# Another order for one hand-written schedule: linear-attention block and ReLU MLP, 542 operations

## The chip, the core and the metric

The kernel runs on one core of a Trainium2 chip. The metric is the device time of one execution in microseconds (us). Engines named below: PE (TensorE matmuls; PEld its weight loads), DVE (VectorE), ACT (ScalarE), POOL (GpSimd) and SP (SyncE, here the one that issues every DMA). Each engine works through its own instructions in the order in which the program emits them; semaphores hold an instruction until what it reads is there and what it overwrites is free.

## The reference

Both stages work on the same x (2048 tokens, 512 features); B_x is not used.

```python
def _A_ref(x, wqkv, wo):                       # 32 heads of 16
    qkv = (x @ wqkv).reshape(B, S, 3, H, Dh).transpose(2, 0, 3, 1, 4)
    q, k, v = qkv[0], qkv[1], qkv[2]
    phi = lambda t: jnp.where(t > 0, t + 1, jnp.exp(t)) + 1e-6
    pq, pk = phi(q), phi(k)
    kv = jnp.einsum("bhsd,bhse->bhde", pk, v)
    z = jnp.einsum("bhsd->bhd", pk)
    num = jnp.einsum("bhqd,bhde->bhqe", pq, kv)
    den = jnp.einsum("bhqd,bhd->bhq", pq, z)[..., None] + 1e-6
    return (num / den).transpose(0, 2, 1, 3).reshape(B, S, D) @ wo

def _B_ref(x, w1, w2):                         # 512 -> 1792 -> 512
    return jnp.maximum(x @ w1, 0) @ w2

h = x + _A_ref(_layernorm(x), wqkv, wo)
h2 = h + _B_ref(_layernorm(h), w1, w2)
```

## The kernel before

The 2048 rows are 16 tiles t of 128, four tiles to a chunk c of 512 columns. The program is a set of small operations (`op_...`) and one string, `ORDER`, with 542 words; a word names an operation and its numbers, and the loop at the end emits them one after another:

```python
for word in ORDER.split():
    name, *idx = word.split(".")
    ops[name](*map(int, idx))
```

So the order of the words is the order on every engine's queue, and nothing else sets it. The last number of a PE word is its PSUM bank of eight.

What the words do, by stage:

- Loads, on SP: `lx.t.n` loads n tiles of x; `lk`, `lq`, `lv`, `lo`, `l1`, `l2` load rows of wk, wq, wv, wo, w1 and w2 (L200 to L211).
- `warm.n.b`: n products of zeros on PE (L215).
- First layernorm: `S.t` and `A.t` on DVE (statistics, L218, L219), `R.t.n` on ACT (1/sqrt as exp of a logarithm, two instructions, L224, L225), `N.t` on DVE (normalise, L243).
- Transposing normalised rows into `lnT`: tiles 0 to 3 with `T.t.b` on PE (L262) and `E.t` on ACT (L272); tiles 4 to 15 with `X.t`, a transposing DMA issued on SP (L283).
- Keys: `K.t.b` on PE (four matmuls, L291), then `F` (exp) and `U` (relu) on ACT (L309, L312) and `M`, `D` on DVE (min, add; L316, L319) make phi(k), one or two tiles at once. `G.t` (four matmuls into banks 4 to 7, L343) sums phi(k)^T ln(x) over all tiles; `za` and `zf` on DVE and `z` on PE sum phi(k).
- Queries: `Q.c.j.b` on PE (four matmuls, L299), `qF`, `qU`, `qM`, `qD` as for the keys.
- `gD` (DVE, L379) or `gA` (ACT, L376) copies G's banks out; `kv`, `kx`, `m` make one 512 by 512 matrix of kv and wo, copied out by `mA` (ACT) or `mD` (DVE).
- Denominators: `dn.c.b` on PE (16 small matmuls, L440), `dnl`, `dnx` on ACT (logarithm and exp, L446, L453), `dt.t`, a transposing DMA on SP (L460), into `rd`, and `dm` on DVE (L464), which multiplies phi(q) by it, two of four feature blocks at once.
- `h.t.b` on PE (four matmuls, L474), `hD.t` on DVE (adds x, L480); second layernorm with `s`, `a`, `n` on DVE (L220, L221, L250) and `r` on ACT; `x.t`, a transposing DMA on SP (L284).
- MLP: `p.c.f.b` on PE (four matmuls, L490), copied out with relu, two f at once, by `pA` (ACT, L496) or `pD` (DVE, L501); `f.t.b.f0.n` on PE (n matmuls of the sum over 14, L510); `fo.t` on DVE (scale and add, L518); `fd.t` on SP (store, L525). The activations lie in `acts[c % 2]`.

For one chunk the path is thus: four `dt` (after `dn`, `dnl`, `dnx`), two `dm`, four `h`, `hD`, `s`, `a`, `n`, four `x`, then `p`.

Of the kernel before, what the change touches and what calls it, by code (L numbers as in the profile page):

```python
# [15 lines left out]


ORDER = """
const lx.0.1 S.0 lx.2.1 S.2 lx.1.1 A.2 A.0 table warm.9.7 R.2.1 S.1 lx.3.1 N.2 A.1 R.0.1 R.1.1 N.0 lx.4.2
warm.1.7 T.2.0 S.3 E.2 N.1 T.0.1 A.3 lk.0.2 lk.2.2 S.4 S.5 A.4 lx.6.2 A.5 T.1.5 E.0 R.3.1 E.1 R.4.2 lx.8.4 N.3  # L20
K.0.3 S.6 N.4 F.0.1 U.0.1 K.1.0 lx.12.4 M.0.1 S.7 N.5 F.1.1 X.4 A.6 D.0.1 M.1.1 A.7 T.3.5 E.3 K.2.3 S.9 U.1.1
F.2.1 R.6.2 K.3.2 G.0 D.1.1 U.3.1 N.7 X.5 S.8 X.7 N.6 A.8 M.2.1 A.9 U.2.1 R.8.2 F.3.1 S.10 D.2.1 G.1 N.8 K.4.0
masks S.11 N.9 A.10 A.11 M.3.1 K.5.1 G.2 X.6 U.4.2 R.10.2 X.8 K.7.3 F.4.2 K.6.2 S.13 D.3.1 X.9 G.3 N.11 S.12
M.4.2 A.12 A.13 N.10 K.8.0 K.9.1 D.4.2 X.11 R.12.2 G.4 F.6.2 N.12 N.13 S.14 U.6.2 S.15 za.2 A.14 A.15 M.6.2
G.5 K.11.3 X.10 U.8.2 F.8.2 K.10.2 R.14.2 X.13 X.12 M.8.2 D.6.2 lq.0.2 lq.2.2 N.14 K.13.1 D.8.2 za.4 K.12.0
U.10.2 F.10.2 M.10.2 N.15 D.10.2 za.6 G.6 U.12.2 F.12.2 X.14 G.7 G.8 Q.0.1.1 Q.0.0.0 X.15 M.12.2 za.8 D.12.2
K.14.2 K.15.3 qU.0.0.2 qF.0.0.2 za.10 G.9 za.12 Q.0.2.0 Q.0.3.1 F.14.2 l1.2.2 M.14.2 U.14.2 zf.12 qF.0.2.2
D.14.2 G.10 G.11 z.0.2.14 z.2.2.14 z.1.2.14 qM.0.2.2 qM.0.0.2 z.3.2.14 qU.0.2.2 qD.0.2.2 lv.2.2 l2.7.7 lv.0.2
zc G.12 qD.0.0.2 G.13 zh dn.0.0 G.14 G.15 dnl.0 dnx.0.2.2 gD.0.2 Q.1.0.2 Q.1.1.3 dnx.0.0.2 gA.2.2 kv.0.4
Q.1.2.0 kv.3.4 Q.1.3.1 kv.2.4 qF.1.0.2 qU.1.0.2 qM.1.0.2 lo.2.2 lo.0.2 kv.1.4 kx Q.2.1.3 qF.1.2.2 dt.2 dt.3  # L30
dt.0 dt.1 qU.1.2.2 m.0.4 m.1.5 m.3.7 m.2.6 Q.2.0.2 qM.1.2.2 mA.0.2 qD.1.0.2 qD.1.2.2 dn.1.5 mA.2.2 dnl.1
dnx.1.2.2 dm.0.0.2 dm.0.2.2 h.3.4 h.2.0 hD.3 s.3 l1.0.2 dnx.1.0.2 hD.2 dt.6 a.3 Q.2.3.1 h.0.5 s.2 dt.4 hD.0
qU.2.0.2 qF.2.0.2 Q.2.2.0 qM.2.0.2 h.1.2 dt.5 dt.7 s.0 n.3 a.2 hD.1 a.0 s.1 n.0 Q.3.1.3 a.1 n.2 qF.2.2.2
qU.2.2.2 qM.2.2.2 dm.1.0.2 Q.3.0.2 dm.1.2.2 n.1 Q.3.3.1 Q.3.2.0 x.3 qF.3.0.2 qU.3.0.2 h.7.4 h.6.5 x.0 x.2
qU.3.2.2 qD.2.2.2 x.1 qD.2.0.2 dn.2.3 dnl.2 qF.3.2.2 h.5.6 h.4.7 hD.7 qM.3.0.2 hD.6 hD.5 s.7 p.0.0.2 p.0.1.3
hD.4 qM.3.2.2 s.6 dnx.2.2.2 dnx.2.0.2 pD.0.0.2 qD.3.2.2 s.4 dt.10 p.0.3.1 p.0.2.0 p.0.4.2 p.0.5.3 pA.0.2.2
pA.0.4.2 qD.3.0.2 dt.8 dt.11 dt.9 dn.3.6 p.0.6.0 p.0.7.1 p.0.13.3 dnl.3 s.5 a.4 p.0.12.2 pA.0.6.2 dnx.3.0.2
pA.0.12.2 r.0.4 dnx.3.2.2 l2.0.7 a.5 n.5 a.7 dm.2.0.2 a.6 n.6 dm.2.2.2 n.7 x.7 h.11.4 h.9.6 h.8.1 h.10.5 hD.11
n.4 hD.9 hD.8 hD.10 x.4 dt.13 dt.12 x.6 x.5 dt.14 dt.15 p.0.10.0 f.2.6.0.7 p.0.11.1 pA.0.10.2 p.0.8.2 p.0.9.3
f.3.7.0.7 pD.0.8.2 s.8 dm.3.0.2 dm.3.2.2 f.2.6.7.7 p.1.0.0 p.1.1.1 f.3.7.7.7 h.12.3 pD.1.0.2 h.14.4 p.1.2.2  # L40
p.1.12.0 hD.12 s.12 fo.3 fo.2 s.10 a.12 s.9 hD.14 s.11 a.9 n.9 h.13.7 f.1.5.0.7 p.1.13.1 h.15.3 a.10 hD.13 a.8
n.10 pD.1.12.2 n.8 hD.15 s.15 p.1.10.6 p.1.11.7 f.0.4.0.7 p.1.3.3 p.1.8.0 f.0.4.7.7 a.15 p.1.9.1 fd.2
f.1.5.7.7 pD.1.2.2 s.13 n.15 pA.1.8.2 fo.1 a.11 n.12 n.11 pD.1.10.2 x.8 x.9 x.10 x.11 p.1.4.0 p.1.5.1 p.1.6.2
r.4.4 p.1.7.3 pA.1.4.2 pA.1.6.2 f.5.5.0.7 p.2.3.3 p.2.8.0 p.2.9.1 f.7.7.0.7 p.2.2.2 pD.2.8.2 fo.0 p.2.1.1
p.2.0.0 f.6.6.0.7 s.14 a.13 n.13 pD.2.2.2 pD.2.0.2 a.14 p.2.7.3 f.4.4.0.7 p.2.12.0 p.2.6.2 f.7.7.7.7 p.2.13.1
n.14 f.5.5.7.7 pD.2.6.2 pA.2.12.2 p.2.5.1 p.2.4.0 x.13 fd.0 fd.3 x.15 fd.1 pA.2.4.2 x.14 x.12 f.4.4.7.7
p.3.0.0 p.3.2.2 p.3.1.1 f.6.6.7.7 p.3.3.3 pA.3.2.2 pD.3.0.2 fo.7 fo.5 fo.6 fo.4 p.3.9.1 f.11.7.0.7 p.2.11.3
fd.4 p.3.8.0 p.2.10.2 f.9.5.0.7 pD.2.10.2 pD.3.8.2 p.3.6.2 p.3.7.3 f.9.5.7.7 f.10.6.0.7 pA.3.6.2 p.3.10.2
p.3.11.3 f.8.4.0.7 fd.6 fd.5 fd.7 p.3.4.0 f.10.6.7.7 p.3.5.1 f.11.7.7.7 f.8.4.7.7 pA.3.4.2 r.12.4 r.8.4
pD.3.10.2 fo.9 fo.10 fo.8 fo.11 p.3.12.0 p.3.13.1 pD.3.12.2 fd.9 fd.8 fd.10 fd.11 f.14.6.0.7 f.13.5.0.7  # L50
f.12.4.0.7 f.14.6.7.7 f.13.5.7.7 f.12.4.7.7 fo.13 fo.14 fo.12 fd.12 fd.14 f.15.7.0.14.0.2 fo.15.0.2
f.15.4.0.14.2.1 f.15.5.0.14.3.1 fo.15.2.1 fo.15.3.1 fd.13 fd.15.0.2 fd.15.2.1 fd.15.3.1
"""


# [505 lines left out]
```

## Time and profile before

| what | us |
|---|---|
| median of 3 runs (lowest, highest) | 171.69 (171.44, 172.59) |
| the profiled execution | 171.47 |
| its span, first to last instruction | 169.8 |
| DVE / ACT busy | 103.3 / 64.9 |
| DMA packets of the program, share of 16 engines | 35.8% |

The page shows each engine's busy time, then the span in 40 slices (a digit is the busy tenths of a slice). These rows of it tell of DMA: the busy share of the 16 DMA engines by slice, and the queues. `q1` carries all that SP issues; `q8` and `q14` carry the fetches of the engines' own instructions, in packets of 16 KB and 8 KB. They run on the same 16 DMA engines.

```profile
DMA  5874466891556434564400131004500210003004
q1 hardware_dynamic: 32224, 15.74, 35.8%
q8 instruction: 6, 0.10, 0.2%
q14 instruction: 4, 0.03, 0.1%
```

By the packet records the six 16 KB packets start at 21.97, 44.68, 63.33, 88.23, 115.85 and 142.85 us and take 0.88 to 1.68 us each on one DMA engine; the 8 KB packets start at 16.62, 43.08, 77.35 and 86.58 and take 0.31 to 0.49.

The timeline of SP with all its transposing DMAs: a line has start, length of the merged stretch, line, kind, tensors and count.

```profile
10.27 14.38 SPq L283 DMA_TRANSPOSE lnT<-h_nat  x10
25.90 3.19 SPq L283 DMA_TRANSPOSE lnT<-h_nat  x2
41.40 6.19 SPq L460 DMA_TRANSPOSE rd<-wk_sb  x4
50.71 5.12 SPq L460 DMA_TRANSPOSE rd<-wk_sb  x4
55.92 5.15 SPq L284 DMA_TRANSPOSE lnT<-hn  x4
```

SP is held about 1.2 us by one transposing DMA, and the median from issue to landing is 2.5 us.

### The profile page before, as it was taken

The page shows a single profiled execution, that of the slowest core. Times are in us where ns is not written, and L with a number is a line of the kernel's source. Part 1 is how long each engine was busy: PE and PEld are TensorE (multiplying, and loading weights), DVE is VectorE, ACT ScalarE, POOL GpSimd, SP SyncE. Part 2 cuts the span into 40 slices and gives each one's busy share as a digit, 9 for nine tenths or more (in the row PEclk, how much of TensorE's full clock was granted, in tenths as well). Part 3 has the DMA queues.
Part 4 walks back from the last instruction along what each step waited for, and adds up shares of the span by engine and source line. Part 5 has one row for each costly group of instructions (what it writes and reads, how often), then busy time and mean ns, then how long its engine had stood idle before and what let it go on. Part 6 is the DMA issues. An engine that isn't in the chain of part 4 may idle for free.

```text
span 169.8 us, 2263 instructions
## 1 busy us (share of the span) xinstructions
PE 162.2 (96%) x843; PEld 75.4 (44%) x858; DVE 103.3 (61%) x206; ACT 64.9 (38%) x97; POOL 4.7 (3%) x21
## 2 busy tenths in 40 slices
PE   7799899999989999999999999999999999999993
...
DVE  3989999995269999770499845093203550227052
...
DMA  5874466891556434564400131004500210003004
GB/s 144 251 253 95 94 95 184 262 359 60 99 174 165 93 66 85 152 173 86 92 6 31 31 62 29 2 0 107 113 0 0 70 54 4 0 0 124 0 4 120
DMA packets 32234, 15.87 MB, mean 93 GB/s; under 512 B 24800, under 2 KB 31200, under 8 KB 32224
## 3 DMA queue, kind: packets, MB, share of 16 engines
q1 hardware_dynamic: 32224, 15.74, 35.8%
q8 instruction: 6, 0.10, 0.2%
q14 instruction: 4, 0.03, 0.1%
HBM read 7.86 MB, written 2.10 MB: 59 GB/s over the span
## 4 chain that ended last, share of the span: by engine, by line
PE 80%; DMA 6%; DVE 6%; SPq 2%; issue 2%; ACT 1%; DVEq 0%
PE bk L510 29%; PE bk L490 28%; PE bk L474 7%; PE bk L343 7%; PE bk L291 5%; PE bk L299 5%; DMA x_nat<-in_A_x_dram 3%; DMA lnT<-h_nat 2%; DVE h_nat L480 2%; DMA rd<-wk_sb 1%; SPq L201 1%; DVE st L220 1%; DVE h_nat L243 1%; PE bk L440 1%; ACT eb L309 1%
## 5 line engine op out<-in xcount | busy, mean ns | idle before, releaser
L510 PE MATMUL bk<-w_sb,at 128*128 128x512 bf16 (+2 forms) x249 | 51.9, 355 | 0.2
L490 PE MATMUL bk<-lnT,w_sb 128*128 128x512 bf16 x219 | 51.8, 379 | 0.2
L496 ACT ACTIVATE at<-bk 128x1024 bf16<-128x1024 f32 x13 | 13.3, 1024 | 70.6 <-PE bk L490 48.7
L501 DVE TENSOR_SCALAR at<-bk 128x1024 bf16<-128x1024 f32 x15 | 18.2, 1220 | 32.5 <-PE bk L490 32.3
L510 PEld LDWEIGHTS <-at 128*128 128x128 bf16 x252 | 23.6, 98 | 25.4 <-ACT at L496 0.3
L490 PEld LDWEIGHTS <-w_sb 128*128 128x128 bf16 x224 | 21.8, 98 | 26.1 <-issue 0.2
L518 DVE SCALAR_TENSOR_TENSOR gT<-bk,rstd,h_nat 128x512 bf16<-128x512 f32 (+2 forms) x18 | 11.7, 685 | 16.0 <-PE bk L510 10.5
L312 ACT ACTIVATE rb<-bk 128x1024 bf16<-128x1024 f32 (+1 forms) x18 | 16.4, 927 | 3.7 <-PE bk L299 2.4
L309 ACT ACTIVATE eb<-bk 128x1024 bf16<-128x1024 f32 (+1 forms) x18 | 16.6, 927 | 3.0 <-PE bk L299 2.8
L291 PE MATMUL bk<-wk_sb,lnT 128*128 128x512 bf16 x63 | 15.6, 379 | 1.3 <-DMA wk_sb<-in_A_wqkv_dram 0.6
L474 PE MATMUL bk<-m_sb,pqs 128*128 128x512 bf16 x61 | 15.0, 379 | 0.9 <-DVE pqs L464 0.8
L299 PE MATMUL bk<-lnT,wq_sb 128*128 128x512 bf16 x64 | 15.6, 379 | 0.2 <-DVE h_nat L480 0.2
L343 PE MATMUL bk<-at,h_nat 128*128 128x512 bf16 x54 | 13.3, 379 | 0.1
L480 DVE TENSOR_TENSOR h_nat<-bk,x_nat 128x512 bf16<-128x512 f32 x16 | 10.9, 681 | 2.0 <-PE bk L474 1.9
L218 DVE BATCH_NORM_STATS2 st<-x_nat 128x6 f32<-128x512 bf16 x16 | 10.6, 674 | 2.4 <-DMA x_nat<-in_A_x_dram 2.4
L220 DVE BATCH_NORM_STATS2 st<-h_nat 128x6 f32<-128x512 bf16 x16 | 11.0, 686 | 0.1
L291 PEld LDWEIGHTS <-lnT 128*128 128x128 bf16 x64 | 5.8, 98 | 9.5 <-DMA lnT<-h_nat 1.8
L474 PEld LDWEIGHTS <-pqs 128*128 128x128 bf16 x64 | 6.0, 98 | 8.0 <-DVE pqs L464 1.5
L299 PEld LDWEIGHTS <-wq_sb 128*128 128x128 bf16 x64 | 6.1, 98 | 7.2 <-issue 0.4
L343 PEld LDWEIGHTS <-h_nat 128*128 128x128 bf16 x64 | 6.1, 98 | 7.1
L316 DVE TENSOR_SCALAR eb<-eb 128x1024 bf16<-128x1024 bf16 (+1 forms) x18 | 6.8, 384 | 2.5 <-ACT eb L309 2.5
L453 ACT ACTIVATE wk_sb<-ld 128x1024 bf16<-128x1024 f32 x8 | 8.1, 1049 | 0.1
...
## 6 DMA issues: line engine op xcount, KB each, us to landing
...
```

Source lines behind the costliest of these rows:

```text
L220: op_s = lambda t: nc.vector.bn_stats(out=st2[:, t, :], in_=h_nat[:, t, :])
L291: nc.tensor.matmul(bk[:, b, :], lhsT=lnT[c][:, kd, j * P : (j + 1) * P], rhs=wk_sb[:, kd, :], start=(kd == 0), stop=(kd == KD - 1),)
L299: nc.tensor.matmul(bk[:, b, :], lhsT=wq_sb[:, kd, j * P : (j + 1) * P], rhs=lnT[c][:, kd, :], start=(kd == 0), stop=(kd == KD - 1),)
L309: nc.scalar.activation(out=buf(eb, kind, i, n), in_=bank(at_bank[kind, i], n), func=ACT.Exp)
L312: nc.scalar.activation(out=buf(rb, kind, i, n), in_=bank(at_bank[kind, i], n), func=ACT.Relu)
L343: nc.tensor.matmul(bk[:, KD + kd, :], lhsT=ln_nat[:, t, kd * P : (kd + 1) * P], rhs=pk(t)[:, 0, :], start=(t == 0), stop=(t == NT - 1),)
L474: nc.tensor.matmul(bk[:, b, :], lhsT=pqs[:, (c * KD + jb) % NQ, j * P : (j + 1) * P], rhs=m_sb[:, jb, :], start=(jb == 0), stop=(jb == KD ...
L480: nc.vector.tensor_tensor(out=h_nat[:, t : t + n, :], in0=bank(at_bank["h", t], n), in1=x_nat[:, t : t + n, :], op=ALU.add,)
L490: nc.tensor.matmul(bk[:, b, cols], lhsT=w1_sb[:, kd, f * P : (f + 1) * P], rhs=lnT[c][:, kd, cols], start=(kd == 0), stop=(kd == KD - 1),)
L496: nc.scalar.activation(out=acts[c % 2][:, f : f + n, :], in_=bank(at_bank["p", c, f], n), func=ACT.Relu)
L501: nc.vector.tensor_scalar(out=acts[c % 2][:, f : f + n, :], in0=bank(at_bank["p", c, f], n), scalar1=0.0, scalar2=None, op0=ALU.max,)
L510: nc.tensor.matmul(bk[:, b, 0 : w * P], lhsT=acts[c % 2][:, f, j * P : (j + 1) * P], rhs=w2_sb[:, f, k * P : (k + w) * P], start=(f == 0), ...
```

## The change

Only the string `ORDER` changes. Both versions have 542 words and the same work. Some copies change engine: `gA.2.2` (ACT) becomes `gD.2.2` (DVE), `mA.2.2` becomes `mD.2.2`, and of the 28 relu copies of the MLP ten go from `pD` to `pA` and four from `pA` to `pD`. Some `T`, `K` and `h` products use other PSUM banks. All else is where the words stand. The whole diff, its unchanged lines left out:

```diff
-const lx.0.1 S.0 lx.2.1 S.2 lx.1.1 A.2 A.0 table warm.9.7 R.2.1 S.1 lx.3.1 N.2 A.1 R.0.1 R.1.1 N.0 lx.4.2
-warm.1.7 T.2.0 S.3 E.2 N.1 T.0.1 A.3 lk.0.2 lk.2.2 S.4 S.5 A.4 lx.6.2 A.5 T.1.5 E.0 R.3.1 E.1 R.4.2 lx.8.4 N.3
-K.0.3 S.6 N.4 F.0.1 U.0.1 K.1.0 lx.12.4 M.0.1 S.7 N.5 F.1.1 X.4 A.6 D.0.1 M.1.1 A.7 T.3.5 E.3 K.2.3 S.9 U.1.1
-F.2.1 R.6.2 K.3.2 G.0 D.1.1 U.3.1 N.7 X.5 S.8 X.7 N.6 A.8 M.2.1 A.9 U.2.1 R.8.2 F.3.1 S.10 D.2.1 G.1 N.8 K.4.0
-masks S.11 N.9 A.10 A.11 M.3.1 K.5.1 G.2 X.6 U.4.2 R.10.2 X.8 K.7.3 F.4.2 K.6.2 S.13 D.3.1 X.9 G.3 N.11 S.12
-M.4.2 A.12 A.13 N.10 K.8.0 K.9.1 D.4.2 X.11 R.12.2 G.4 F.6.2 N.12 N.13 S.14 U.6.2 S.15 za.2 A.14 A.15 M.6.2
-G.5 K.11.3 X.10 U.8.2 F.8.2 K.10.2 R.14.2 X.13 X.12 M.8.2 D.6.2 lq.0.2 lq.2.2 N.14 K.13.1 D.8.2 za.4 K.12.0
-U.10.2 F.10.2 M.10.2 N.15 D.10.2 za.6 G.6 U.12.2 F.12.2 X.14 G.7 G.8 Q.0.1.1 Q.0.0.0 X.15 M.12.2 za.8 D.12.2
-K.14.2 K.15.3 qU.0.0.2 qF.0.0.2 za.10 G.9 za.12 Q.0.2.0 Q.0.3.1 F.14.2 l1.2.2 M.14.2 U.14.2 zf.12 qF.0.2.2
-D.14.2 G.10 G.11 z.0.2.14 z.2.2.14 z.1.2.14 qM.0.2.2 qM.0.0.2 z.3.2.14 qU.0.2.2 qD.0.2.2 lv.2.2 l2.7.7 lv.0.2
-zc G.12 qD.0.0.2 G.13 zh dn.0.0 G.14 G.15 dnl.0 dnx.0.2.2 gD.0.2 Q.1.0.2 Q.1.1.3 dnx.0.0.2 gA.2.2 kv.0.4
-Q.1.2.0 kv.3.4 Q.1.3.1 kv.2.4 qF.1.0.2 qU.1.0.2 qM.1.0.2 lo.2.2 lo.0.2 kv.1.4 kx Q.2.1.3 qF.1.2.2 dt.2 dt.3
-dt.0 dt.1 qU.1.2.2 m.0.4 m.1.5 m.3.7 m.2.6 Q.2.0.2 qM.1.2.2 mA.0.2 qD.1.0.2 qD.1.2.2 dn.1.5 mA.2.2 dnl.1
-dnx.1.2.2 dm.0.0.2 dm.0.2.2 h.3.4 h.2.0 hD.3 s.3 l1.0.2 dnx.1.0.2 hD.2 dt.6 a.3 Q.2.3.1 h.0.5 s.2 dt.4 hD.0
-qU.2.0.2 qF.2.0.2 Q.2.2.0 qM.2.0.2 h.1.2 dt.5 dt.7 s.0 n.3 a.2 hD.1 a.0 s.1 n.0 Q.3.1.3 a.1 n.2 qF.2.2.2
-qU.2.2.2 qM.2.2.2 dm.1.0.2 Q.3.0.2 dm.1.2.2 n.1 Q.3.3.1 Q.3.2.0 x.3 qF.3.0.2 qU.3.0.2 h.7.4 h.6.5 x.0 x.2
-qU.3.2.2 qD.2.2.2 x.1 qD.2.0.2 dn.2.3 dnl.2 qF.3.2.2 h.5.6 h.4.7 hD.7 qM.3.0.2 hD.6 hD.5 s.7 p.0.0.2 p.0.1.3
-hD.4 qM.3.2.2 s.6 dnx.2.2.2 dnx.2.0.2 pD.0.0.2 qD.3.2.2 s.4 dt.10 p.0.3.1 p.0.2.0 p.0.4.2 p.0.5.3 pA.0.2.2
-pA.0.4.2 qD.3.0.2 dt.8 dt.11 dt.9 dn.3.6 p.0.6.0 p.0.7.1 p.0.13.3 dnl.3 s.5 a.4 p.0.12.2 pA.0.6.2 dnx.3.0.2
-pA.0.12.2 r.0.4 dnx.3.2.2 l2.0.7 a.5 n.5 a.7 dm.2.0.2 a.6 n.6 dm.2.2.2 n.7 x.7 h.11.4 h.9.6 h.8.1 h.10.5 hD.11
-n.4 hD.9 hD.8 hD.10 x.4 dt.13 dt.12 x.6 x.5 dt.14 dt.15 p.0.10.0 f.2.6.0.7 p.0.11.1 pA.0.10.2 p.0.8.2 p.0.9.3
-f.3.7.0.7 pD.0.8.2 s.8 dm.3.0.2 dm.3.2.2 f.2.6.7.7 p.1.0.0 p.1.1.1 f.3.7.7.7 h.12.3 pD.1.0.2 h.14.4 p.1.2.2
-p.1.12.0 hD.12 s.12 fo.3 fo.2 s.10 a.12 s.9 hD.14 s.11 a.9 n.9 h.13.7 f.1.5.0.7 p.1.13.1 h.15.3 a.10 hD.13 a.8
-n.10 pD.1.12.2 n.8 hD.15 s.15 p.1.10.6 p.1.11.7 f.0.4.0.7 p.1.3.3 p.1.8.0 f.0.4.7.7 a.15 p.1.9.1 fd.2
-f.1.5.7.7 pD.1.2.2 s.13 n.15 pA.1.8.2 fo.1 a.11 n.12 n.11 pD.1.10.2 x.8 x.9 x.10 x.11 p.1.4.0 p.1.5.1 p.1.6.2
-r.4.4 p.1.7.3 pA.1.4.2 pA.1.6.2 f.5.5.0.7 p.2.3.3 p.2.8.0 p.2.9.1 f.7.7.0.7 p.2.2.2 pD.2.8.2 fo.0 p.2.1.1
-p.2.0.0 f.6.6.0.7 s.14 a.13 n.13 pD.2.2.2 pD.2.0.2 a.14 p.2.7.3 f.4.4.0.7 p.2.12.0 p.2.6.2 f.7.7.7.7 p.2.13.1
-n.14 f.5.5.7.7 pD.2.6.2 pA.2.12.2 p.2.5.1 p.2.4.0 x.13 fd.0 fd.3 x.15 fd.1 pA.2.4.2 x.14 x.12 f.4.4.7.7
-p.3.0.0 p.3.2.2 p.3.1.1 f.6.6.7.7 p.3.3.3 pA.3.2.2 pD.3.0.2 fo.7 fo.5 fo.6 fo.4 p.3.9.1 f.11.7.0.7 p.2.11.3
-fd.4 p.3.8.0 p.2.10.2 f.9.5.0.7 pD.2.10.2 pD.3.8.2 p.3.6.2 p.3.7.3 f.9.5.7.7 f.10.6.0.7 pA.3.6.2 p.3.10.2
-p.3.11.3 f.8.4.0.7 fd.6 fd.5 fd.7 p.3.4.0 f.10.6.7.7 p.3.5.1 f.11.7.7.7 f.8.4.7.7 pA.3.4.2 r.12.4 r.8.4
-pD.3.10.2 fo.9 fo.10 fo.8 fo.11 p.3.12.0 p.3.13.1 pD.3.12.2 fd.9 fd.8 fd.10 fd.11 f.14.6.0.7 f.13.5.0.7
-f.12.4.0.7 f.14.6.7.7 f.13.5.7.7 f.12.4.7.7 fo.13 fo.14 fo.12 fd.12 fd.14 f.15.7.0.14.0.2 fo.15.0.2
-f.15.4.0.14.2.1 f.15.5.0.14.3.1 fo.15.2.1 fo.15.3.1 fd.13 fd.15.0.2 fd.15.2.1 fd.15.3.1
+const lx.2.1 S.2 lx.0.1 lx.1.1 S.0 S.1 A.0 A.1 A.2 lx.4.2 table lx.3.1 R.0.1 S.3 N.0 R.2.1 R.1.1 A.3 R.3.1
+warm.9.7 N.1 N.2 warm.1.7 N.3 T.0.6 S.5 lk.0.2 lk.2.2 S.4 T.1.3 T.2.4 E.0 T.3.1 K.0.7 A.5 lx.6.2 A.4 E.1 E.2
+E.3 R.4.2 F.0.1 S.7 S.6 K.1.4 F.1.1 K.3.2 N.4 K.2.1 N.5 A.7 M.1.1 M.0.1 A.6 U.0.1 U.1.1 R.6.2 D.0.1 F.2.1
+D.1.1 N.7 N.6 lx.8.4 lx.12.4 U.2.1 F.3.1 S.8 S.9 X.4 X.5 M.3.1 A.8 M.2.1 A.9 X.6 G.0 G.1 K.4.0 U.3.1 D.3.1
+D.2.1 X.7 R.8.2 K.5.1 G.2 N.9 X.9 G.3 K.6.2 U.4.2 F.4.2 K.7.3 N.8 S.10 S.12 S.13 A.12 M.4.2 A.13 R.12.2 K.9.1
+F.6.2 X.8 U.6.2 S.14 S.11 N.12 D.4.2 A.11 A.10 M.6.2 N.13 X.12 X.13 K.8.0 R.10.2 F.8.2 D.6.2 G.4 N.10 A.14
+S.15 N.11 X.10 X.11 A.15 za.2 M.8.2 U.8.2 lq.0.2 lq.2.2 G.5 za.4 D.8.2 masks G.6 G.7 K.12.0 K.13.1 R.14.2 N.15
+X.15 za.6 N.14 za.8 U.12.2 F.12.2 K.10.2 K.11.3 G.8 F.10.2 U.10.2 M.12.2 M.10.2 D.10.2 G.9 X.14 Q.0.1.1
+Q.0.0.0 D.12.2 za.10 qF.0.0.2 qU.0.0.2 K.14.2 K.15.3 G.10 Q.0.2.0 za.12 zf.12 U.14.2 F.14.2 M.14.2 Q.0.3.1
+G.11 G.12 qF.0.2.2 D.14.2 qU.0.2.2 z.0.2.14 z.1.2.14 z.2.2.14 z.3.2.14 qM.0.0.2 qM.0.2.2 qD.0.2.2 G.13 zc
+qD.0.0.2 lo.2.2 lv.0.2 l2.0.7 lv.2.2 l1.0.2 lo.0.2 zh G.14 dn.0.0 G.15 dnl.0 gD.0.2 gD.2.2 dnx.0.2.2 Q.1.1.3
+Q.1.0.2 dnx.0.0.2 Q.1.2.0 qF.1.0.2 kv.1.4 dt.3 qU.1.0.2 Q.1.3.1 qM.1.0.2 qF.1.2.2 kv.2.4 kv.0.4 kv.3.4 Q.2.1.3
+qD.1.0.2 kx m.0.4 m.1.5 m.3.7 m.2.6 dt.1 dt.2 dt.0 qU.1.2.2 qM.1.2.2 Q.2.0.2 qD.1.2.2 mD.2.2 dm.0.0.2 mA.0.2
+dn.1.5 Q.2.3.1 dm.0.2.2 h.3.7 hD.3 dnl.1 h.0.6 s.3 dnx.1.2.2 l1.2.2 h.2.5 Q.2.2.0 hD.0 h.1.6 dt.7 dnx.1.0.2
+qU.2.0.2 qF.2.0.2 Q.3.0.2 Q.3.1.3 hD.2 qF.2.2.2 qU.2.2.2 a.3 s.0 s.2 n.3 a.0 a.2 hD.1 n.0 n.2 dt.5 dt.6 dt.4
+s.1 dm.1.0.2 x.3 dm.1.2.2 x.2 x.0 qM.2.0.2 a.1 Q.3.2.0 Q.3.3.1 n.1 qF.3.0.2 qU.3.2.2 qF.3.2.2 qU.3.0.2
+qM.2.2.2 qD.2.0.2 qD.2.2.2 h.7.7 h.5.4 h.6.6 h.4.5 dn.2.3 dnl.2 x.1 p.0.0.2 hD.7 hD.5 qM.3.2.2 hD.6 s.7 hD.4
+p.0.1.3 dnx.2.2.2 dnx.2.0.2 p.0.2.0 p.0.3.1 pA.0.0.2 qM.3.0.2 a.7 qD.3.2.2 pA.0.2.2 p.0.5.3 p.0.4.2 pA.0.4.2
+r.0.4 s.4 qD.3.0.2 n.7 l2.7.7 dt.11 s.6 dt.10 dt.8 dt.9 dn.3.6 p.0.7.1 p.0.6.0 pA.0.6.2 dnl.3 a.6 s.5 dm.2.0.2
+a.4 p.0.12.2 p.0.13.3 a.5 n.5 dm.2.2.2 pA.0.12.2 p.0.10.0 f.2.6.0.7 p.0.11.1 dnx.3.2.2 n.4 pD.0.10.2 n.6
+dnx.3.0.2 r.4.4 x.5 dt.14 x.7 dt.13 dt.12 dt.15 x.4 x.6 p.0.9.3 p.0.8.2 h.11.7 pA.0.8.2 h.9.4 h.10.2 f.1.5.0.7
+f.1.5.7.7 f.2.6.7.7 h.8.3 p.1.1.1 p.1.0.0 dm.3.0.2 hD.11 hD.9 hD.10 fo.2 dm.3.2.2 s.9 s.10 fo.1 hD.8 pA.1.0.2
+p.1.2.2 h.13.7 h.15.4 hD.13 h.14.5 p.1.13.1 p.1.12.0 pD.1.12.2 p.1.3.3 f.3.7.0.7 s.13 pD.1.2.2 h.12.0 s.11
+hD.15 hD.14 a.10 a.11 hD.12 s.8 n.11 a.8 a.9 f.3.7.7.7 f.0.4.0.7 p.1.9.1 p.1.8.0 p.1.6.2 p.1.10.6 p.1.7.3
+pA.1.8.2 fd.2 fd.1 r.8.4 s.15 n.8 s.12 a.13 a.12 n.10 n.13 fo.3 s.14 n.9 pD.1.6.2 a.14 p.1.5.1 p.1.4.0
+p.1.11.7 f.0.4.7.7 x.8 pA.1.4.2 x.10 x.9 x.11 fd.3 n.14 pD.1.10.2 fo.0 f.7.7.0.7 p.2.2.2 p.2.8.0 p.2.3.3
+f.4.4.0.7 p.2.9.1 pA.2.8.2 pD.2.2.2 f.5.5.0.7 p.2.1.1 p.2.7.3 f.7.7.7.7 f.4.4.7.7 f.6.6.0.7 p.2.0.0 p.2.6.2
+pA.2.0.2 f.6.6.7.7 p.2.4.0 a.15 fo.7 n.12 pD.2.6.2 p.2.5.1 p.2.11.3 r.12.4 pA.2.4.2 fo.6 fd.0 f.11.7.0.7
+p.2.10.2 p.2.13.1 p.2.12.0 pA.2.12.2 fo.4 n.15 fd.7 x.14 x.15 fd.4 x.13 x.12 f.5.5.7.7 f.8.4.0.7 p.3.9.1
+p.3.8.0 fo.5 pA.2.10.2 pA.3.8.2 fd.5 fd.6 p.3.2.2 f.10.6.0.7 p.3.4.0 f.9.5.0.7 p.3.3.3 p.3.5.1 f.10.6.7.7
+pA.3.4.2 p.3.1.1 pD.3.2.2 p.3.6.2 f.11.7.7.7 p.3.0.0 p.3.7.3 f.9.5.7.7 pD.3.6.2 pA.3.0.2 p.3.10.2 f.8.4.7.7
+p.3.11.3 p.3.13.1 fo.10 fo.11 fo.9 f.13.5.0.7 f.14.6.0.7 p.3.12.0 pA.3.12.2 pA.3.10.2 fo.8 f.12.4.0.7
+f.13.5.7.7 f.14.6.7.7 fd.8 fd.11 fd.10 fd.9 f.12.4.7.7 fo.13 fo.12 fo.14 f.15.7.0.14.0.2 f.15.5.0.14.3.1
+fo.15.0.2 fd.13 fd.12 fd.14 fd.15.0.2 fo.15.3.1 f.15.4.0.14.2.1 fo.15.2.1 fd.15.3.1 fd.15.2.1
```

## The prediction

> **What bounds the kernel now.** First the page: the busy time and the slices.
>
> ```profile
> PE 162.2 (96%) x843; PEld 75.4 (44%) x858; DVE 103.3 (61%) x206; ACT 64.9 (38%) x97; POOL 4.7 (3%) x21
> PE   7799899999989999999999999999999999999993
> DVE  3989999995269999770499845093203550227052
> ```
>
> PE is the bound, and from slice 15 (4.24 us each) it is full. All that an order can win lies before that, so I read next PE's timeline from 5 to 57 us, the lines with idle time in front of them:
>
> ```profile
> 6.98 0.40 PE L262 MATMUL bk<-ident,h_nat 128*128 128x128 bf16 x4 [0.52 <-DVE h_nat L243]
> ...
> 8.54 1.46 PE L291 MATMUL bk<-wk_sb,lnT 128*128 128x512 bf16 x6 [0.63 <-DMA wk_sb<-in_A_wqkv_dram]
> ...
> 18.03 1.04 PE L291 MATMUL bk<-wk_sb,lnT 128*128 128x512 bf16 x4 [0.52 <-DMA lnT<-h_nat]
> ...
> 49.84 1.84 PE L474 MATMUL bk<-m_sb,pqs 128*128 128x512 bf16 x7 [0.81 <-DVE pqs L464]
> ...
> 56.16 1.02 PE L299 MATMUL bk<-lnT,wq_sb 128*128 128x512 bf16 x4 [0.16 <-DVE h_nat L480]
> ```
>
> The brackets count from the modelled end of the last matmul. By start-to-start times (a 512-column matmul follows the last after 0.216 us, so K, Q, G, h or p, four each, cost 0.864) the waits are 0.68 (T.1), 0.79 (K.0 for its weights), 0.37 (K.2, K.3), 0.68 (K.6), 0.17 (K.12), 1.11 (h.3), 0.32 (Q.3.0): 4.1 us between T.2 at 5.68 and p.0.0 at 62.62. After p.0.0 there is none (steps of twice 0.216 every 50 matmuls are missing records). Of these, 1.96 hang on a transposing DMA (K.6, K.12, h.3).
>
> Third, the chain of waits from 43 to 50 us, and the DMA answers for one microsecond and one transpose there:
>
> ```profile
> 45.33 0.94 SPq L460
> 46.28 0.04 issue
> 46.32 2.47 DMA rd<-wk_sb
> 48.79 0.03 DVEq L464
> 48.82 0.05 issue
> 48.87 0.70 DVE pqs L464
> 49.57 0.27 issue
> 49.84 0.38 PE bk L474
> ```
>
> ```profile
> q8 instruction: 1, 0.02, 7.3%
> ```
>
> ```profile
> rd<-wk_sb SPq DMA_TRANSPOSE x1, 4.3
> ```
>
> The second fence is the microsecond from 44.5: one 16 KB instruction packet, 7.3% of 16 engines' 1.0 us, so 1.17 us on one of them. The third is dt.3, issued at 42.63: 4.3 us to landing where the median is 2.5. dt.0 behind it (43.99) holds SP 2.28 us instead of 1.2, so dt.1 goes out 1.05 late, lands at 48.79, and PE idles. The same at 21.97 (X.10 4.1 us, X.13 2.08 on SP) and, smaller, at 16.62 with an 8 KB packet (X.6 3.39). A 16 KB packet costs a train of transposes about 1.0 us, an 8 KB one about 0.9 to one landing. The 16 KB packets follow PE's instruction count: 276 PE records (137 matmuls, 139 loads) between the first two, then 229, 259, 254. The change keeps PE's counts, so they stay within a product or so of the same place.
>
> **The change part by part.** I follow each engine's own new queue, with start-to-start times of DVE and ACT from the rows: S 0.60, A 0.10, N 0.32, one-tile M 0.17 and D 0.32, two-tile M 0.32 and D 0.60, za 1.14; one-tile F, U, E 0.48, two-tile 0.92, R 0.45.
>
> *Start: costs 1.4 us at T, returned in part.* lx.3 moves behind lx.4.2 and S.3 stands ahead of N.0 on DVE. Before, those 768 KB had landed at 6.06, so lx.3 lands then (earliest 4.73, its time before). Behind the waiting S.3 are N.0 to N.3, hence all transposes: N.0 6.69, T.0 7.12 (before 5.68), N.3 7.76, T.3 8.17. K.0 needs wk_sb, landed 8.50 in an unchanged place, so it starts at 8.40 without its wait, and K.1, K.3, K.2 follow gapless to 11.86, against K.3's end at 12.16. S.7 and S.6 now precede N.4: X.4 issues at 11.1 (before 10.27). E.3 and a later R.4 precede F.0 on ACT, so D.0 ends at 12.27 and G.0 waits 0.44. X.5 and X.6 go out at 12.4 and 13.7, both ahead of the 8 KB packet, which moves with DVE's count to about 16.5; X.7 (15.0) takes its 0.9, lands about 18.4, and K.7 is wanted at 18.34. K.6's 0.68 is gone.
>
> *X.12 to X.11.* N.12 follows S.12, S.13, S.14, S.11: X.12 at 20.15, X.13 21.6, X.10, X.11. PE's packet, in the middle of G.4, comes at 21.4 and still meets them. Bounds for X.11's landing: 26.2 (not hit) and 27.9 (X.10's and X.13's delays both in full); I take 27.2, one packet's 1.0. Now G.4 to G.7, K.12 and K.13 stand ahead: K.11 is wanted at 27.0 and waits 0.2. lq is issued after X.11, near 26.1, landing by its own 3.1 at 29.8, when Q.0.1 is wanted: cover used up, any slip is paid in full.
>
> *G.15 to h.3.* zh ends at 39.6, dn.0 starts 39.7. gD.2.2 on DVE (1.22) in place of gA on ACT (1.00) ends at 43.4, just ahead of kv.1; mD.2.2 ends at 48.4 ahead of dm.0.0: both nothing, covered by Q products; uncovered, 1.2 each. The train dt.3, dt.1, dt.2, dt.0 goes out at 41.75, 43.0, 44.3 and, with a packet near 44.7, 46.6; dt.0 lands at 49.05 (48.0 not hit, 49.9 hit as X.10 was). h.3 starts at 49.85, but one more product, Q.2.3, is done: PE waits 0.7 + 0.16, not 1.11. The 0.32 at Q.3.0 goes: h.1 is in bank 6, not in bank 2 that Q.3.0 needs. dm.1.0 stands behind s.1 on DVE and h.7 waits 0.1.
>
> *Loads.* lo, lv, l2.0, l1.0 in a new order carry the same 2.9 MB as before (29.14 to 40.27), from 30.0: done about 41.2; lv is wanted at 43.4, lo at 46. l1.2.2 moves behind dt.0 (lands near 53, wanted at 62) and l2.7.7 to 61 (lands 66, wanted at 81). Nothing; dt.7 waits for ACT anyway.
>
> *MLP part.* Covered evacuations everywhere, with four places at no slack: p.0.5 after pA.0.0, f.7 after pD.1.10, p.3.10 after pD.3.6, f.13's second half after pA.3.10, which now stands behind pA.3.12. An evacuation is 1.02 (ACT) or 1.22 us (DVE). Bounds 0 and 1.0 each; I take 0.15 together. Last f, fo and fd mirror two columns: nothing.
>
> *Sum.* PE work from the first T to p.0.0 is 62.62 - 5.68 - 4.12 = 52.82. After: 7.12 + 52.82 + waits (T 0.39, G.0 0.44, X 0.26, h.3 0.86, h.7 0.10) = 62.0, 0.6 earlier; less 0.15 makes 0.45. Span 169.8 - 0.45 = 169.35. The profiled execution took 171.47, 1.67 around its span: 171.0; the median of the runs is 0.22 above it: 171.2.
>
> The Trainium skill ("Runtime: NRT & Kernel Launch", Instruction fetch mechanics) says that the sequencer fetches the next block by itself and that crossing a block is mostly hidden. The trace disagrees: dt.1 went out 1.05 us late beside such a packet. By that rule there is nothing to place around, and the result would be the second rival's.
>
> **The rivals.**
>
> 1. *The trains miss the packets and lx.3 comes early.* If lx.3 lands by 5.4, all behind DVE moves up to 0.6; if dt's order also clears the packet, h.3's 0.86 goes. Against it: four transposes at 1.3 us fill more than the time around a packet. 171.2 - 0.6 - 0.86 = 169.7. Chance 0.22.
>
> 2. *It does not do what it says.* The late landings have another cause than the packets and come back elsewhere: K.6's 0.68 and h.3's 1.11 return in full, against 0.26 and 0.86 in my sum: +0.67, so 171.9. Against it: of six transposes that a 16 KB packet overlapped, five landed 0.8 to 1.9 us late (dt.10 only 0.2). Chance 0.14.
>
> 3. *Slower: the clock.* PE now idles from the last warm product's end near 5.5 to 7.1, where before T.2 began at 5.68. The warm products ran at 0.427 us each, later ones at 0.216, and after the last matmul the clock fell back within 2.6 us (the window 166.9 to 169.7 shows 0.95 granted). If 1.6 us of silence and sparse T products suffice, K and G run at half rate for as long as the warm ones did (about 4 us): 2.0 us, 173.2. It decides if the clock falls before 8.4. Against: before, 5.6 to 8.5 was nearly as thin and stayed at 1.00. Chance 0.09. The Trainium skill ("TensorE: Matmul & The Clock Gate", Part 1) puts the return to half clock after an idle window of about 3.4 us; by that the 1.6 us are safe, and no run here shows the limit.
>
> 4. *A tie goes to the waiting side.* DVE and ACT are in order; where an evacuation misses by one instruction, 0.6 to 1.2 us are paid, at lq or the four MLP places: two of them, 172.7. Chance 0.15.
>
> **How the numbers follow.** My forecast has 0.40, with its own range 170.4 to 171.8 (X and dt bounds of ±0.8, damped by what follows). 1% is 1.7 us, what a measurement can tell from no change: below 170.0 counts as faster, above 173.4 as slower. Faster is most of rival 1: 0.20. Slower is half of rivals 3 and 4: 0.12. Same: 0.68. The range 169.6 to 173.0 leaves one in ten on either side.
>
> **What would show it.** Right: T.0 near 7.1 waiting for DVE behind lx.3; no idle time at K.0 and K.6; h.3 behind Q.2.3 with under 1 us before it; p.0.0 near 62.0; no PE gap after it. Wrong: matmuls 0.427 us apart after 8 us; Q.0.1 waiting on wq_sb; PE waits on L496 or L501 after 62 us; transposes landing in 2.5 us beside a 16 KB packet.

## The result, and the profile after

The changed kernel takes 172.6 us (median of 13 executions, 172.16 to 173.08), the kernel before 171.46 in the same comparison (13, 171.07 to 172.59): ratio 1.0059, interval 1.004 to 1.0079. It is about 1.0 us slower; 171.2 was forecast. Executions over 1.5% above the fastest of the same kernel are left out of every ratio and average in this document. The profiled execution took 172.49 with a span of 170.78, against 171.47 and 169.76.

The page, its rows of busy time and slices, and the clock's:

```profile
PE 163.0 (95%) x843; PEld 75.8 (44%) x858; DVE 98.6 (58%) x202; ACT 69.7 (41%) x101; POOL 4.7 (3%) x21
PE   7599999999999989999999999999999999999993
PEclk9879999999999999999999999999999999999999
```

PE is as full as before from the third slice on. New is the last row: the granted clock is below 9 in the second and third slices (4.3 to 12.8 us). PE's timeline has, from 4 to 64 us, these four lines with idle time in front:

```profile
6.71 1.74 PE L262 MATMUL bk<-ident,h_nat 128*128 128x128 bf16 x16 [1.78 <-DVE h_nat L243]
28.47 1.04 PE L291 MATMUL bk<-wk_sb,lnT 128*128 128x512 bf16 x4 [0.27 <-DMA lnT<-h_nat]
51.03 2.93 PE L474 MATMUL bk<-m_sb,pqs 128*128 128x512 bf16 x12 [0.34 <-DVE pqs L464]
63.54 0.81 PE L490 MATMUL bk<-lnT,w_sb 128*128 128x512 bf16 x3 [0.46 <-DMA lnT<-hn]
```

K.6's wait is gone, h.3's is 0.66 by start-to-start times (1.11 before), Q.3.0's is gone: PE waits less, as forecast. But the last line is new: p.0.0 itself waits for the last of four `x`, 0.6 us. And the stretches of the start (length, PE, PEld, DVE, ACT, POOL, clock, DMA share, GB/s):

```profile
5.60:8.50 2.90, 1.79 (x17) 1.39 (x18) 2.85 (x8) 2.40 (x9) 0.51 (x2) 0.82 0.93 300
8.50:12.00 3.50, 3.50 (x12) 1.36 (x11) 2.56 (x8) 2.34 (x7) 0.00 (x0) 0.67 0.57 212
```

The clock records grant full speed from 4.02 to 7.43, half to 10.84, then full; K's matmuls stand 0.427 us apart. G.0 starts at 13.17 (before 12.16, forecast 12.3). Two parts of the chain of waits show what follows:

```profile
45.18 0.92 ACT rb L312
46.11 0.20 SPq L460
46.30 0.05 issue
46.35 1.27 SPq L460
47.62 0.05 issue
47.67 2.23 DMA rd<-wk_sb
...
60.82 2.47 DMA lnT<-hn
63.29 0.25 issue
63.54 0.59 PE bk L490 x2
```

The first part still holds the `dt` train and its packet (44.79, 1.08 us; dt.3 takes 3.98 us, dt.0 lands at 50.20, forecast 49.05). The last part was not in the chain of before: x.1, issued at 60.82, lands at 63.29 and starts p.0.0. From p.0.0 to PE's end it is 104.37 us, before 104.26. So nearly the whole loss, 0.92 of the 1.02 in the span, lies ahead of p.0.0. G.0 is already 1.01 late, and from G.0 to p.0.0 it takes 50.37 us, before 50.46: in this execution the loss is there before G.0 starts.

### The path that sets p.0.0

SP's timelines after show why x.1 comes when it does:

```profile
43.03 5.90 SPq L460 DMA_TRANSPOSE rd<-wk_sb  x4
51.65 5.12 SPq L460 DMA_TRANSPOSE rd<-wk_sb  x4
56.86 5.17 SPq L284 DMA_TRANSPOSE lnT<-hn  x4
```

There are two trains. The first, dt.0 to dt.3, meets the 16 KB packet and leads to h.3. The second, eight transposes of 1.3 us without a gap between, leads to x.1, and no 16 KB packet meets it in either kernel. From its first issue to p.0.0 it is 11.9 us in both (50.71 to 62.62, 51.65 to 63.54). Its first transpose reads what `dnx.1` on ACT writes, and it overwrites a part of `rd`, which the two `dm` of the first train's chunk on DVE must have read. So it waits for both. Here is ACT between dn.0 and that point, before:

```profile
39.91 0.37 ACT L446 ACTIVATE ld<-bk,eps 128x128 f32<-128x128 f32 x1 [2.30 <-PE bk L440]
40.31 2.00 ACT L453 ACTIVATE wk_sb<-ld 128x1024 bf16<-128x1024 f32 x2
42.22 1.00 ACT L376 ACTIVATE gT<-bk 128x1024 bf16<-128x1024 f32 x1
...
47.40 1.94 ACT L399 ACTIVATE m_sb<-bk 128x1024 bf16<-128x1024 f32 x2
49.22 0.37 ACT L446 ACTIVATE ld<-bk,eps 128x128 f32<-128x128 f32 x1
49.63 2.00 ACT L453 ACTIVATE wk_sb<-ld 128x1024 bf16<-128x1024 f32 x2
```

and after:

```profile
41.55 0.37 ACT L446 ACTIVATE ld<-bk,eps 128x128 f32<-128x128 f32 x1 [2.30 <-PE bk L440]
41.95 2.00 ACT L453 ACTIVATE wk_sb<-ld 128x1024 bf16<-128x1024 f32 x2
...
48.17 1.02 ACT L399 ACTIVATE m_sb<-bk 128x1024 bf16<-128x1024 f32 x1
49.85 0.37 ACT L446 ACTIVATE ld<-bk,eps 128x128 f32<-128x128 f32 x1 [0.65 <-PE bk L440]
50.25 2.00 ACT L453 ACTIVATE wk_sb<-ld 128x1024 bf16<-128x1024 f32 x2
```

ACT hardly rests between dn.0's logarithm and dnx.1. With two copies fewer (gA.2, mA.2) the first half of dnx.1 ends 10.33 us behind dn.0's start (51.30) instead of 11.35 (50.68). The two `dm` on DVE, before and after:

```profile
48.87 1.29 DVE L464 TENSOR_TENSOR pqs<-pqT,rd 128x1024 bf16<-128x1024 bf16 x2 [0.62 <-DMA rd<-wk_sb]
...
50.28 1.29 DVE L464 TENSOR_TENSOR pqs<-pqT,rd 128x1024 bf16<-128x1024 bf16 x2 [0.38 <-issue]
```

Before, they end at 50.16 and ACT at 50.68, and the train starts at 50.71. After, ACT ends at 51.30 but the `dm` only at 51.57, and the train starts at 51.65: now the first train's last landing and the `dm` behind it release the second train. It is so in all seven profiles of the changed kernel below, with or without added products; where the order behind dn.0 is before's, it is ACT in all eight. The way from dn.0 to the second train is thus 10.68 us instead of 11.38; 0.70 of ACT's 1.02 are won. But dn.0 starts at 40.97 instead of 39.33: +1.64 - 0.70 = +0.94, and p.0.0 is 0.92 later. Of the 1.64, 1.01 are there at G.0, from the start, where the clock fell in this execution. The other 0.63 arise between G.0 and dn.0, where one more product (G.14, 0.86) stands ahead of dn.0. What each is worth in time was the question for the experiments.

Two theories. **A**: the clock, which falls more readily in the changed start. **B**: the order up to dn.0, because dn.0's time sets p.0.0.

### The profile page after: what moved, and what is told of

It is laid out like the page before. It is cut to its first block, busy times and chain, and to the rows that moved or that the text cites. A ratio compares the mean times of both kernels' runs of the same rounds, so it can differ in the third digit from the quotient of the medians.

```text
span 170.8 us, 2259 instructions
## 1 busy us (share of the span) xinstructions
PE 163.0 (95%) x843; PEld 75.8 (44%) x858; DVE 98.6 (58%) x202; ACT 69.7 (41%) x101; POOL 4.7 (3%) x21
## 4 chain that ended last, share of the span: by engine, by line
PE 77%; DVE 9%; DMA 6%; ACT 2%; SPq 2%; issue 2%
PE bk L490 29%; PE bk L510 28%; PE bk L474 6%; PE bk L299 5%; PE bk L343 4%; PE bk L291 3%; DVE st L218 3%; DMA x_nat<-in_A_x_dram 2%; DVE h_nat L243 2%; DMA lnT<-h_nat 1%; DMA lnT<-hn 1%; ACT eb L309 1%; DMA rd<-wk_sb 1%; ACT rb L312 1%; DVE at L319 1%
## 5 line engine op out<-in xcount | busy, mean ns | idle before, releaser
L510 PE MATMUL bk<-w_sb,at 128*128 128x512 bf16 (+2 forms) x247 | 50.8, 355 | 0.2
L496 ACT ACTIVATE at<-bk 128x1024 bf16<-128x1024 f32 x19 | 19.2, 1024 | 72.2 <-PE bk L490 60.0
L501 DVE TENSOR_SCALAR at<-bk 128x1024 bf16<-128x1024 f32 x9 | 11.0, 1223 | 28.0 <-PE bk L490 28.0
L291 PE MATMUL bk<-wk_sb,lnT 128*128 128x512 bf16 x63 | 16.2, 404 | 0.4 <-DMA lnT<-h_nat 0.3
L299 PE MATMUL bk<-lnT,wq_sb 128*128 128x512 bf16 x62 | 14.8, 379 | 0.1
L480 DVE TENSOR_TENSOR h_nat<-bk,x_nat 128x512 bf16<-128x512 f32 x16 | 10.4, 677 | 0.8 <-PE bk L474 0.7
L291 PEld LDWEIGHTS <-lnT 128*128 128x128 bf16 x64 | 6.4, 104 | 9.1 <-DMA lnT<-h_nat 1.5
L464 DVE TENSOR_TENSOR pqs<-pqT,rd 128x1024 bf16<-128x1024 bf16 x8 | 5.3, 686 | 8.2 <-DMA rd<-wk_sb 7.8
```

The source lines that it names most:

```text
L291: nc.tensor.matmul(bk[:, b, :], lhsT=lnT[c][:, kd, j * P : (j + 1) * P], rhs=wk_sb[:, kd, :], start=(kd == 0), stop=(kd == KD - 1),)
L299: nc.tensor.matmul(bk[:, b, :], lhsT=wq_sb[:, kd, j * P : (j + 1) * P], rhs=lnT[c][:, kd, :], start=(kd == 0), stop=(kd == KD - 1),)
L496: nc.scalar.activation(out=acts[c % 2][:, f : f + n, :], in_=bank(at_bank["p", c, f], n), func=ACT.Relu)
L501: nc.vector.tensor_scalar(out=acts[c % 2][:, f : f + n, :], in0=bank(at_bank["p", c, f], n), scalar1=0.0, scalar2=None, op0=ALU.max,)
L510: nc.tensor.matmul(bk[:, b, 0 : w * P], lhsT=acts[c % 2][:, f, j * P : (j + 1) * P], rhs=w2_sb[:, f, k * P : (k + w) * P], start=(f == 0), ...
```

## The experiments

Each ratio is to runs of the kernel before on the same chip, with its 95% interval. "Up to w" below means: the first kernel's order up to the word w, then the other's order for all words that are left.

### Which part loses

`front_after`: the changed order up to Q.0.0 and D.12, then before's. `front_before`: the reverse, seam at Q.0.1.

```diff
 X.14 Q.0.1.1 Q.0.0.0 D.12.2
-za.10 qF.0.0.2 qU.0.0.2 K.14.2
+K.14.2 K.15.3 qU.0.0.2 qF.0.0.2
...
```

> The changed order up to Q.0.1, then the rest of the words in the old order. If the front alone is to blame (clock and the late X.10, X.11): p.0.0 near 63.4, time 172.2 to 172.6. If the middle (G.10 ahead of Q.0.2, the late dt train, x.1) is: within 0.3 of the old kernel's 171.5. If each has its part: 171.8 to 172.1.

> The old order up to Q.0.1, then the rest of the words in the changed order. Front to blame: the old kernel's time or up to 0.4 less (Q.2.3 covers part of the wait at h.3, and Q.3.0 no longer waits), 171.0 to 171.5. Middle to blame: 172.2 to 172.6, with p.0.0 waiting for x.1.

front_after: 1.0063 (1.0032 to 1.0093); its profile lost the clock too (half from 7.89 to 11.30), dn.0 at 41.20, p.0.0 23.34 behind it, at 64.54. Of the 1.87 by which its dn.0 is late, 1.27 are there at G.0 (13.43). front_before: 1.0028 (0.9993 to 1.0063), dn.0 at 40.15 although its start was undisturbed (G.0 11.83); here G.14 stands ahead of dn.0. The front shows a loss, the rest none beyond its interval, though the two intervals overlap. Both have dn.0 late.

`start_after`: the changed order up to G.0, then before's. `end_after`: before's up to s.7 ahead of p.0.0, then the changed one.

```diff
 hD.6 hD.5 s.7
+l2.0.7
 p.0.0.2
-p.0.1.3 hD.4 qM.3.2.2
+qM.3.2.2 hD.4
...
```

> The old order up to p.0.0, the changed order from there. MLP part: if its evacuations without slack cost what the prediction took, 0.15 over the old kernel (0 to 0.3), with p.0.0 at 62.6 and PE's end 104.3 to 104.6 us behind it; if ties go to the waiting side there, 0.6 or more.

> The changed order up to G.0 (T and K products, loads, S.3 ahead of N.0), the old order from there. Clock theory: as the grant falls, K at half rate and G.0 near 13.2 in an execution where it falls badly (before 5.2 or after 6.5), 12.2 otherwise; p.0.0 0.5 to 1.0 later than the old kernel's in the first case, within 0.3 in the second; over the rounds 0.4 to 0.9 slower. If the front's later part (X.12, lq) is to blame and not its start: within 0.3 of the old kernel whatever the clock.

end_after: 1.0014 (0.9988 to 1.004), PE's end 104.45 behind p.0.0. start_after: 1.0011 (0.9971 to 1.0051), p.0.0 at 62.68. Neither end alone loses a measurable amount. But five of the ten executions of start_after have a mean clock of 0.99, as front_after's profile with its fall has, and these average a span of 171.28 against 170.24 for the other five: the changed start costs when the clock falls in it. Whether the rest of front_after's loss is the order between G.0 and Q.0.0 isn't shown; G.14 does not stand ahead of dn.0 there.

### The clock

`after_second_look`: the changed kernel again, once. 

> The changed order once more, unaltered. Clock theory: whether the K products run at half rate hangs on the moment at which the clock was first granted; if this execution gets it after 5.3 us, no fall, K products 0.216 apart, G.0 near 12.2, p.0.0 near 62.8, span 169.9 to 170.2; if it gets it before 5 us, the fall comes back with G.0 near 13.2 and a span of 170.6 to 171.0. Order theory: G.0 and the span do not go with the clock.

173.24 us, span 170.6. Here the clock was not lost but granted late, at 10.37 us; the result for K is the same, G.0 13.16, p.0.0 63.21.

`after_warm`: the changed kernel with the array kept busy in the wait ahead of T.0 by five more 512-column products of zeros. `after_tiny`: five one-column products instead, which move PE's instruction count as far but leave the array nearly idle.

```diff
-warm.9.7 N.1 N.2 warm.1.7 N.3 T.0.6
+warm.9.7 N.1 N.2 warm.6.7 N.3 T.0.6
```

```diff
+    def op_tiny(n, b):
+        for _ in range(n):
+            nc.tensor.matmul(bk[:, b, 0:1], lhsT=zeros[:, 0:P], rhs=ones[:], start=True, stop=True)
-N.1 N.2 warm.1.7 N.3 T.0.6
+N.1 N.2 warm.1.7 tiny.5.7 N.3 T.0.6
```

> The changed order with six warm products in place of one ahead of T.0 (five more products of zeros). Clock theory (the idle PE ahead of T.0 lets the clock fall to half for the first K products, which puts G.0 0.9 late and all behind it): K products 0.216 us apart, G.0 near 12.3 instead of 13.17, time 0.7 to 1.0 below the changed order's 172.6, so 171.6 to 171.9. Order theory (the clock's loss is hidden, DVE's and ACT's order sets the end): within 0.2 of 172.6 though the K products are fast.

> The changed order with five one-column products behind the warm ones: PE's instruction count is moved by ten, as with the longer warm-up, but the array stays idle. Clock theory: still half rate, 172.6 within 0.2. Fetch theory (what counts is where the 16 KB packets fall): the packets come about 1 us earlier in the order, and if that alone moves the time by over 0.4, the gain of the longer warm-up is not the clock's.

Both profiles had full speed in the start: G.0 at 12.16 and 12.14, p.0.0 at 62.93 and 62.68. The times did not follow: 1.0035 (1.0003 to 1.0066) and 1.0069 (1.0034 to 1.0103). after_warm's PE timeline shows the other thing that the forecast had missed in the start:

```profile
20.82 1.04 PE L291 MATMUL bk<-wk_sb,lnT 128*128 128x512 bf16 x4 [0.72 <-DMA lnT<-h_nat]
```

The 8 KB packet came at 19.43, not at 16.5; it hit X.8 (3.37 us to landing), and K.8 waited 0.89 by start-to-start times. With the clock up, dn.0 is thus at 40.23, forecast 39.7.

`before_short_warm`: the kernel before with fewer zero products, to provoke the clock there.

```diff
-table warm.9.7 R.2.1 S.1
+table warm.4.7 R.2.1 S.1
```

> The old order with four warm products in place of nine, so that PE idles from about 3.4 to T.2 at 5.7, and all else old. Clock theory: T and K products at half rate (0.427 us) until about 9 to 10.5, G.0 at 12.7 to 13.2 instead of 12.16, p.0.0 0.4 to 0.9 later, time 0.4 to 0.9 over the old kernel. If the half rate at the start is hidden behind loads and DVE: G.0 and the time as before within 0.2.

1.0053 (1.0022 to 1.0084): the clock was granted only at 10.98, G.0 13.43, p.0.0 63.69, 1.07 later than before. So a slow start is carried to the end in before's order as well.

In a last comparison of this kind, on one chip: `before_fill`, the changed kernel unaltered (`after_timed`) and `after_warm` a second time (`after_warm_again`, edit above).

```diff
-lx.6.2 A.5 T.1.5 E.0 R.3.1 E.1 R.4.2 lx.8.4 N.3 K.0.3
+lx.6.2 A.5 warm.2.7 T.1.5 E.0 R.3.1 E.1 R.4.2 lx.8.4 N.3 warm.2.7 K.0.3
```

> The kernel before with two products of zeros put ahead of T.1 and two ahead of K.0, in the places where PE waits 0.68 and 0.79 us, so that the array is never idle for long between 5.6 and 8.5 us. Nothing else moves. Theory A (in many executions the clock falls in the start, and each fall costs 0.5 to 1.4 us): with the idle time filled the clock can't fall; p.0.0 at 62.6 us in the profile as before, and the ratio of the times 0.2 to 0.5% below 1. Theory B (before hardly ever loses its clock, and what the changed order costs is its order): ratio 1.000, within 0.2%. If the filling itself delays T.1 or K.0, p.0.0 comes up to 0.4 later and the ratio is up to 1.002.

> The changed kernel unaltered, timed beside the one with more zero products. Both theories: 1.004 to 1.008. A profile in which the clock falls or is granted late has p.0.0 at 63.2 to 63.6 us (theory A); one in which it does neither has it near 62.8, so 0.2 later than before and not earlier (theory B's part, and what the prediction's 62.0 missed).

> The changed kernel with six products of zeros instead of one behind N.2, as measured once (1.0035), now beside the unaltered changed kernel. Theory A (most of the loss is the clock): 1.000 to 1.003, and at least 0.4% below the unaltered one; profile with p.0.0 near 62.9. Theory B (the order up to dn.0 costs it: dn.0 one product later, and p.0.0 follows dn.0 by a fixed 22.6 us): 1.003 to 1.006, within 0.2% of the unaltered one.

before_fill 1.0002 (0.997 to 1.0035), after_timed 1.0039 (1.0006 to 1.0073), after_warm_again 1.0064 (1.003 to 1.0098). Theory A asked for filled kernels that are 0.2 to 0.5% faster than unfilled ones; neither is. The filling is not a clean test, though: the added products also move PE's instruction count and with it the 16 KB packets (second one at 42.48 in after_warm, 44.79 in the changed kernel). after_timed's profile had the late grant (10.56; p.0.0 63.42). after_warm_again had the clock from 5.49 and was late by something else:

```profile
9.80 3.18 PE L291 MATMUL bk<-wk_sb,lnT 128*128 128x512 bf16 x14 [0.94 <-DMA wk_sb<-in_A_wqkv_dram]
```

The second half of wk landed at 9.76 instead of the 7.9 to 8.9 of the other profiles, and that delay too reached p.0.0 (64.22).

### The packets and lq

`q_early`: after_warm with lq issued ahead of X.12, the Q products ahead of G.9 and dn.0 ahead of G.14, to bring dn.0 back to 39.4.

```diff
-N.13 X.12 X.13
+N.13 lq.0.2 lq.2.2 X.12 X.13
...
-D.10.2 G.9 X.14 Q.0.1.1 Q.0.0.0
+D.10.2 Q.0.1.1 Q.0.0.0 G.9 X.14
...
-K.15.3 G.10 Q.0.2.0 za.12 zf.12 U.14.2 F.14.2 M.14.2 Q.0.3.1 G.11
+K.15.3 Q.0.2.0 za.12 zf.12 U.14.2 F.14.2 M.14.2 Q.0.3.1 G.10 G.11
...
-zh G.14 dn.0.0 G.15
+zh dn.0.0 G.14 G.15
```

> The changed order with six warm products ahead of T.0, lq issued ahead of X.12 (where SP idles), Q.0.1 and Q.0.0 one product earlier (ahead of G.9), Q.0.2 and Q.0.3 ahead of G.10, dn.0 ahead of G.14. Middle theory (p.0.0 waits for x.1, which follows dn.0 at a fixed distance of 22.5 us): dn.0 near 39.4 instead of 40.2, dt.0 landing near 48.8, x.1 near 61.9, p.0.0 near 62.1, span 169.5 to 169.8, 0.6 to 0.9 less than with the longer warm-up alone. If PE's own work and not that chain is the bound: span unchanged at 170.4.

A miss: 1.0107 (1.0064 to 1.0149). Behind the two loads and beside the 16 KB packet (22.69) X.12 took 5.3 us to land (25.65); beside the packet alone it took 4.13 in after_warm. K.12 waited for it, and dn.0 came at 40.50.

`fetch_moved`: after_warm with eight one-column products ahead of Q.0.2, which bring PE's instruction count, and with it the packet, forward.

```diff
-K.14.2 K.15.3 G.10 Q.0.2.0
+K.14.2 K.15.3 G.10 tiny.8.0 Q.0.2.0
```

> The changed order with six warm products ahead of T.0 and eight one-column products ahead of Q.0.2 (0.2 us of PE work), which bring PE's second 16 KB packet 16 instructions, about 1.7 us, earlier: from 42.5 to about 40.8, ended before dt.3 is issued at 42.3. Fetch theory: dt.3 to dt.0 land in 2.5 us each at 1.3 us steps, dt.0 near 48.9 instead of 49.6, h.3's wait under 0.2, p.0.0 near 62.3, span about 169.9 (0.5 less than the longer warm-up alone). If the packets are not what holds the train: dt.0 still 7.2 us behind dt.3's issue and the span 0.2 longer, 170.6.

The 16 KB packet came at 41.84, ahead of the train: dt.3 and dt.1 land in 2.41 us each. But an 8 KB packet at 48.52 met dt.0 (3.12 us), and the tiny products moved dn.0 to 40.63. p.0.0 stands 22.35 behind dn.0, 0.35 less than in after_warm, at 62.98, and the time is 1.0033 (0.9998 to 1.0068). What the first train won, the later dn.0 took back, and in this profile a seventh 16 KB packet (166.01) held up the last stores: the span ended 3.70 behind PE, 2.88 before. So the run doesn't show what a first train clear of packets is worth.

### dn.0 at before's time

`late_cut`: before's order through dn.0, then the changed one (l1.0.2 and l2.0.7 placed later). `late_cut_old_mlp`: the same, but from p.0.0 on before's order again. `late_cut_fill`: that with before_fill's two pairs of zero products.

```diff
 G.13 zh dn.0.0
-G.14 G.15 dnl.0 dnx.0.2.2 gD.0.2 Q.1.0.2
+lo.2.2 lo.0.2 G.14 G.15 dnl.0 gD.0.2 gD.2.2 dnx.0.2.2 Q.1.1.3
...
```

> The old order up to and with dn.0, the changed order behind it (the six large loads keep their old places beside the trains). Chain theory (p.0.0 waits for x.1, and the way from dn.0 over ACT and two trains of transposes to x.1 has no slack in either kernel; it took 23.3 us in the old kernel and 22.5 to 22.7 in the changed one): dn.0 near 39.4, p.0.0 near 61.9 to 62.1, span 169.2 to 169.4, 0.3 to 0.6 less than the old kernel. If PE's own products were the bound, p.0.0 stays at 62.6 and the time at the old kernel's.

> As late_cut up to p.0.0, and the old order from there. Chain theory: p.0.0 as in late_cut, PE's end 104.3 us behind it, 0.4 to 0.7 less than the old kernel in all. If the MLP part of the changed order costs as the prediction took (0.15), it is that much faster than late_cut; if not, the same.

> A mixture meant to beat both: before's order through dn.0 and from p.0.0 on, the changed order between (dn.0 to p.0.0 takes 22.9 instead of 23.3 us there), with the same two pairs of zero products in the start as in the first kernel of this group. If dn.0's time plus the shorter way sets p.0.0 and the clock stays up: p.0.0 near 62.2, span 169.4, ratio 0.996 to 0.998. If the mixture's gain is not real: 1.000, as without the zero products (1.0008).

1.0007 (0.9974 to 1.004), 1.0008 (0.9979 to 1.0037) and 1.0041 (0.9999 to 1.0083). With dn.0 where before's order has it, the changed middle costs nothing measurable in two of three, but nor is it a version that beats both: dn.0 to p.0.0 is 0.1 to 0.4 us shorter than before's 23.29, and 0.1 to 0.7 come back behind p.0.0. In late_cut's profile the clock fell, with before's own start (half from 8.94 to 12.36, G.0 at 13.86):

```profile
8.50:12.00 3.50, 3.04 (x11) 1.39 (x11) 2.70 (x9) 1.87 (x5) 0.00 (x0) 0.56 0.63 257
```

So the clock also falls without the changed start.

### dn.0 alone

`dn_late` and `dn_later`: the kernel before with one word moved, dn.0 behind one more product or two.

```diff
-G.13 zh dn.0.0 G.14 G.15 dnl.0
+G.13 zh G.14 dn.0.0 G.15 dnl.0
```

```diff
-G.13 zh dn.0.0 G.14 G.15 dnl.0
+G.13 zh G.14 G.15 dn.0.0 dnl.0
```

> The kernel before with one word moved: dn.0 stands behind G.14 instead of ahead of it, so it comes one product (0.86 us) later, at 40.2 us, as the changed order has it. Nothing else moves. Theory B (dn.0's time sets p.0.0, since everything between, dt, dm, h, hD, s, a, n, x, is one chain without slack): p.0.0 at 63.4 to 63.6 instead of 62.62, span 170.6, ratio 1.004 to 1.006, which would be all of the loss that the changed kernel shows. Theory A (its loss is the clock's): the train of transposing DMAs has slack or moves past a packet, p.0.0 within 0.2 of 62.6, ratio within 0.2% of 1.

> The same with dn.0 behind G.15, two products later than before (41.1 us). Theory B: p.0.0 at 64.2 to 64.5, span 171.4, ratio 1.008 to 1.012, twice the other's. Theory A: within 0.3% of 1. A third way: the first product costs and the second does not, or the reverse, where the train passes behind PE's instruction packet near 44.7 us (dt.1 then no longer waits for it): ratio 1.003 to 1.006 for both.

1.0049 (1.0015 to 1.0082) and 1.0107 (1.0059 to 1.0155): of 172.05 us that is 0.84 for one product and 1.84 for two. SP's timeline of dn_late:

```profile
42.22 5.62 SPq L460 DMA_TRANSPOSE rd<-wk_sb  x4
51.50 5.14 SPq L460 DMA_TRANSPOSE rd<-wk_sb  x4
56.74 5.15 SPq L284 DMA_TRANSPOSE lnT<-hn  x4
```

dn.0 is 0.82 later (40.15). The first train is 0.82 later as well but is held less by the packet, so that h.3 starts at 49.92, just 0.08 later than before. ACT ends the first half of dnx.1 at 51.48, the second train is 0.79 later and x.1 lands 0.81 later (63.15); p.0.0 is at 63.20, 0.58 later and a little short of the 63.4 that theory B gave. In before's order it is thus not h.3 but the way over ACT and the second train that carries dn.0 to the end. (Another 0.64 are lost behind p.0.0 in that profile, in front of h products at 73.28 that wait for dm.) dn_later's profile lost the clock as well (half from 8.59 to 12.00, G.0 at 13.50, p.0.0 at 65.06), so its time tells more than its profile.

### The clock, counted

Each execution of these comparisons left its span and mean granted clock. The four profiles with a fall have a mean clock of 0.989 to 0.990, and no execution lies between 0.990 and 0.994, so all at 0.990 or below are counted as falls. Of 137 executions of the kernel before, 19 are; their spans average 171.31 us, the other 118 average 170.08. A fall goes with 1.22 us more, in the kernel before too.

With the changed start falls are more frequent: 14 of 44 executions, against 29 of 200 with before's, counting kernels with their zero products as they were. With 512-column products of zeros added in the start there is none in 61, with one-column products 3 in 11. So filling PE's idle time did keep the clock; it did not bring the time down.

Leaving executions with a fall out, the spans average: changed kernel 170.64 (12) and 170.74 (5), after_warm 171.01 (12) and 171.24 (12), dn_late 170.90 (10), dn_later 171.98 (4), before_fill 170.13 (12). The changed order is 0.6 to 1.2 longer without any recorded fall; before's own order with dn.0 one product later is 0.8 longer.

What is shown is that dn.0's time reaches the end: moving dn.0 alone gives a loss of the changed kernel's size, and in all 20 profiles p.0.0 stands 22.35 to 23.34 us behind dn.0, while dn.0 itself lies between 39.00 and 42.04. What makes dn.0 late in the changed kernel is only in part shown. For B speak the extra product, the changed kernel's loss without a recorded fall, and two of three mixtures that keep dn.0 in its place and lose nothing. For A speaks this: the three profiles of the unaltered changed kernel have G.0 0.99 to 1.01 late, after a fall or a late grant, and from G.0 to p.0.0 they take 50.05 to 50.37 us, no longer than before's 50.46 or the 50.26 of before_short_warm, where the grant was late too. With full speed in the start, G.0 is on time and that way takes 50.77 (after_warm) and 50.54 (after_tiny), so that the order's own part in the profiles is 0.31 and 0.06 at p.0.0. Those two profiles have spans of 170.44 and 169.91, below the averages of their own kernels without a fall, 171.01 and 171.15 (8). What makes the usual execution there 0.6 to 1.2 us longer than the profiled one was not seen. In the unaltered kernel a clock granted late is a candidate, since nothing is recorded ahead of the first grant and the mean doesn't sort such executions out.

## Why the prediction failed

- **The end of the chain (the failed step).** The sum followed PE alone: work from T to p.0.0 plus PE's waits, h.3's the largest, and its chain stopped at h.3. It took p.0.0 to be ready when PE is. In the profile after, PE was free for p.0.0 at 62.9 and waited to 63.54 for x.1, the end of the second train, which the first train and its `dm` had released. What PE gained at h.3 and Q.3.0 it gave back there. Before, the two ways met: x.1 landed at 62.34, 0.28 ahead of p.0.0, of which dn_late shows 0.05 to be what the start takes. The sum had dn.0 at 39.7, 0.4 later than before's 39.33, and p.0.0 0.6 earlier, 22.3 behind it; no profile has under 22.35.
- **What this step was worth.** p.0.0 came at 63.54, 1.54 behind the forecast. With the forecast's own landing of dt.0 (49.05), the 1.45 that passed from there to the second train and its 11.89, p.0.0 would stand near 62.4: 0.4 of the 1.54 is the missing way. The other 1.15 is dt.0 itself, landed at 50.20, behind a dn.0 that came 1.27 late; 0.87 of that is G.0, where the clock fell in this execution. What the usual execution lost in place of a fall stays open.
- **G.15 to h.3.** The train was forecast at 41.75, 43.0, 44.3, 46.6 and went at 43.03, 44.32, 46.35, 47.67; dt.0 at 49.05, landed 50.20; three of the four and the landing 1.1 to 1.3 late, behind a dn.0 that came 1.27 behind the forecast. h.3 behind Q.2.3, with 0.66 before it: right (0.86 forecast). h.7: 0.09, right (0.1).
- **"Both nothing" for gD.2 and mD.2.** Too low, in the other direction: off ACT they end dnx.1's first half 1.02 sooner behind dn.0, and 0.70 of it arrives at the second train. That is why the changed kernel does not lose more.
- **The start.** T.0 at 6.71, lx.3 landed at 5.62 (forecast 7.12 and 6.06): between the sum and rival 1's first half, which needed 5.4; it bought nothing. K.0 without its wait: right. G.0 at 12.3: right where the clock stayed up (12.14, 12.16), 0.87 too early in the profiled execution. The 8 KB packet was put at 16.5, by DVE's count, and came at 20.5 (19.4 with full speed); 52 instructions of DVE are recorded ahead of it before and 59 after, so that count does not place it. K.8's 0.89 in after_warm was not in the sum.
- **X.12 to X.11.** PE's packet came at 23.16 (forecast 21.4), X.11 landed at 28.43, beyond the bound of 27.9, since N.12 and X.12 were 0.9 late behind the slow start. K.11 waited 0.43 (0.2), lq landed at 31.01 just before Q.0.1 at 31.07: no cover left, as said, and no wait either, as Q.0.1 follows G.9 without a gap.
- **Loads and MLP.** Nothing and 0.15; measured 104.37 against 104.26 behind p.0.0. Right.
- **Rivals.** The third (clock, 0.09) was given too little: its sign, matmuls 0.427 us apart after 8 us, is in the profiled execution, and a fall or a late grant showed in four of the ten profiles with the changed start, all four among the five without added products, and in three of ten with before's, one of these with zero products taken away. A fall goes with 1.22 us, not 2.0, and happens in before's order too, though less often. The Trainium skill ("TensorE: Matmul & The Clock Gate", Part 1) puts the return to half clock after an idle window of about 3.4 us. The trace shows a fall after a stretch that was partly busy, 4.02 to 7.43, in which PE idled from 4.94 to 6.71. The fourth had the right time (172.7) by another mechanism: no evacuation wait of that size shows behind p.0.0. The second falls, since K.6's and h.3's waits did not return in full and transposes clear of the packet landed in 2.41 us (fetch_moved). Packets that delay the first train do count in the changed kernel, where it releases the second; how much is not shown.
